# One core, Fourier transform and two expert layers: two-operand work on one engine, both width sums on TensorE, layer 1 of all tiles before layer 2

## The chip, the cores and the metric

The kernel runs on 1 core of one Trainium2 chip. The metric is device time in microseconds (us); the kernel before takes 1074.73 us (median of 3 runs, 1071.64 to 1076.15). The engines are TensorE (PE; PEld is its weight load), VectorE (DVE), ScalarE (ACT), GpSimd (POOL) and SyncE (SP, which only issues DMAs here).

## The reference

```python
X = np.fft.fft(np.fft.fft(x, axis=1), axis=2).real      # x: 8 x 3072 x 256
x = X.reshape(8 * 3072, 256)
logits = x @ w_gate                                     # 8 experts
e = argmax(logits); gate = softmax(logits)[e]
# each expert takes its first 768 tokens (capacity), in order; the others give 0
h = relu(disp @ w1[e])          # 256 -> 1024, 8 x 768 rows
y = h @ w2[e]                   # 1024 -> 256
x = gate * y   (0 for tokens that were dropped)
out = max(0.01 * (x @ w_in), x @ w_in) @ w_out          # 256 -> 2048 -> 256
```

All is float32 (w_in and w_out come as float64). Rows of dropped tokens are zero. The kernel multiplies in split form: each factor is a high part and a low part (`x - high`), and each product is three matmuls. So every matrix needs a copy by ScalarE (the high part) and a subtraction (the low part), `split`.

## The kernel before, in words

*Transform stage.* With these inputs the capacities are full after 2.5 of the 8 batches, so only three batches are transformed (`NSTAT = 3`; for the third only half the rows). For each batch `fold_steps` adds and subtracts rows and columns of x that share a table entry (three pieces of rows, j = 0 to 2, each with steps `a0`, `a1`, `b0`), `fsplit_steps` splits the result, `s1_steps` does the transform along the length (TensorE, banks evacuated by `s1_ev_odd` and `s1_ev_even`), and `s2_steps` the transform along the width in 12 chunks of 128 rows. A chunk gives a row block `yd` and its mirror image `ym`; U is the cosine sum and V the sine sum, `yd = U - V` and `ym = U + V`. Three ways are in the code: mode "v" makes U and V by 4 + 3 matmuls of 264 columns and lets VectorE form difference and sum out of PSUM; mode "p" lets TensorE accumulate U - V in one bank and U + V in another, with 14 matmuls, and ScalarE copies both out; mode "d" makes `yd` alone. Before, `PEW` gives mode "p" to 4 chunks of batch 0 and 6 of batch 1; the other 14 of these two batches are "v". Rows with their gate logits go to a table in DRAM (`y_first`). `route` then finds expert, position and slot of each token (one-hot products of `hot` and `place`).

*Expert stage* (`moe_static`). 8 experts x 2 tiles of 384 tokens make 16 tiles. Layer 1 of a tile: `prep` gathers its rows by indirect DMA (POOL queue), `tr` transposes them, `h` (8 steps of 6 matmuls of 384 columns) and `y` (2 steps of 24). Layer 2 of a tile: `h2` and `o`, 16 steps each, then `fin` scatters the rows. Expert weights are loaded by SP and split by `conv_w1` and `conv_w2`; `wide_steps` turns w_in and w_out (float64, as bit patterns) into split form in 16 slices of 512 columns, and must be done before the first `h2`. `zero_step` writes zeros into the output (48 DMAs of 512 KB, on SP).
Before, `lead = 6` tiles go through layer 1, with the wide slices beside them; from then on layer 2 of tile i runs with layer 1 of tile i + 6 in between (`HS`, `W1S` and `W2S` say at which step), and the last 6 tiles have layer 2 alone. The results `yf` of layer 1 wait in 6 SBUF buffers (`my`).

*Who does two-operand work.* `tt` takes VectorE unless it is told another engine; `on(kind, key)` chooses between VectorE and POOL by `SWAP`. In the transform stage POOL takes, of the fold, mostly the column differences (`d`, `q`), the step `b0` for j < 2 and the small edge rows; and a part of the table and evacuation splits and the product with `cid` in `hot`. In the expert stage it takes two of the three two-operand instructions of each wide slice (the third in some slices) and a part of the weight splits.

*Order.* SP runs in the order written, and in `moe_static` ScalarE too; the other engines' order is set by the planner at build time, from its own time model and the data that each instruction needs. `step(pe, own, fn)` runs a step and then takes background steps from a list (`bg`) as far as the credit goes: each step adds its TensorE time `pe` less `own`, each background step has a price (the number beside it).

```python
def split(self, hi, lo, src, eng=None):        # before
    self.act(hi, src)
    self.tt(lo, src, hi, ALU.subtract, eng)
...
self.later([(c * 1.6, f) for c, f in steps])   # the wide slices, beside layer 1
...
self.step(6 * U, 0.5, lambda: self.h(i, f))
```

Of the kernel before, what the change touches and what calls it, by code (L numbers as in the profile page):

```python
# [144 lines left out]
class Kern:  # L145

    SWAP = {
        "tab": ((2, 1),),
        "fold": ((1, 1, "q"), (2, 0, "c"), (2, 1, "b"), (2, 1, "e"), (2, 2, "a")),
        "fs": ((1, 0),),  # L150
        "s1o": ((0, "c", 0), (0, "s", 0), (1, "c", 1), (2, "c", 1), (2, "s", 1)),
        "wd": ((12,), (14,), (4,)),
        "wl": ((5,),),
        "w1": ((1, 1), (1, 2), (1, 3), (2, 0), (2, 2)),
        "w2": ((0, 2), (0, 3), (2, 0), (2, 2), (3, 1), (3, 2), (4, 2)),
    }

    def __init__(self, tc, cap, a):
        self.tc, self.nc, self.a = tc, tc.nc, a
        self.cap = cap  # L160
        self.lead = 6
        self.nt = max(1, -(-cap // T))
        self.capp = self.nt * T
        self.ntab = E * self.capp
        self.slots = self.gq = None
        self.bg, self.credit = [], 0.0

    def on(self, kind, *key, usual="V"):

        v = (usual == "V") != (key in self.SWAP[kind])  # L170
        return self.nc.vector if v else self.nc.gpsimd
# [29 lines left out]
    def tt(self, o, x, y, op, eng=None):  # L201
        (eng or self.nc.vector).tensor_tensor(out=o, in0=x, in1=y, op=op)  # L202
# [4 lines left out]
    def split(self, hi, lo, src, eng=None):  # L207
        self.act(hi, src)
        self.tt(lo, src, hi, ALU.subtract, eng)
# [49 lines left out]
    def build_tables(self, tmp, yp, nb):  # L259
# [5 lines left out]
        for i, n in enumerate("csn"):  # L265
            self.split(self.mv[n + "h"][:, :D], self.mv[n + "l"][:, :D], f[:, i], nc.gpsimd)
# [52 lines left out]
    def load_table(self, pt, j):  # L319

        nc, a = self.nc, self.a
        st = []
        h = TJ // 2
        for i in range(2):
            t = pt.tile([P, h], F32, name="tst", tag=("pch", "pcl", "psh", "psl")[2 * (j % 2) + i])
            o = j * TJ + i * h
            nc.sync.dma_start(out=t, in_=a["tab"][:, o:o + h])
            st.append((1.2, lambda t=t, o=o, i=i: self.split(self.th[:, o:o + h], self.tl[:, o:o + h], t,
                                                             self.on("tab", j, i, usual="VG"[i]))))
        return st  # L330
# [25 lines left out]
    def fold_steps(self, b, pool2=True, pool3=False):  # L356


        nc, tmp = self.nc, self.tmp
        V, G = nc.vector, nc.gpsimd  # L360
        def en(op, j, d):
            return self.on("fold", bkey(b), j, op, usual=d)

        def copy(o, x):
            (G if pool3 else V).tensor_copy(out=o, in_=x)
# [4 lines left out]
        def extra():  # L370
# [3 lines left out]
            tt(t[:, :D], xe[:, 0], xe[:, 1], A, G)  # L374
            tt(xe[:, 0], xe[:, 0], xe[:, 1], M, G)
            tt(c7, c7, x4, A, G)
            tt(o7, xe[:, 0, :P], xe[:, 0, P:], M, G)
            loc["c7"], loc["o7"], loc["x4"] = c7, o7, x4

        def fix():  # L380
            ce, r, c7 = loc["ce", 0], loc["r"], loc["c7"]
            tt(r[0:1, 4, 0], ce[0:1, 0], c7, M, G)
            tt(r[0:1, 5, 0], ce[0:1, 0], c7, A, G)
            copy(loc["x4"], ce[0:1, 1])

        def a0(j):
# [8 lines left out]
            tt(e, x[:, :, :P], x[:, :, P:], A, en("e", j, "V"))  # L395
            tt(x[:, :, :P], x[:, :, :P], x[:, :, P:], M, en("d", j, "G"))
            tt(q, x[:, 0::2, :P], x[:, 1::2, :P], M, en("q", j, "G"))
            if not pool3:
                self.next_x()

        def a1(j):
            e, r = loc["e"], loc["r"]
            c = e[:, 0::2]
            tt(c, c, e[:, 1::2], A, en("c", j, "V"))
            ce = tmp.tile([P, 2, P], F32, name="ce", tag="ce")
            loc["ce", j] = ce
# [8 lines left out]
        def b0(j):  # L415
            if pool3:
                self.next_x()
            Z = en("b", j, "G" if pool3 and j < 2 else "V")
            o, r = loc["o", j], loc["r"]
            se = tmp.tile([P, 2, P], F32, name="se", tag="se")  # L420
            tt(se, o[:, 0::2], o[:, 1::2], M, Z)
            tt(r[:, 2:4, j], o[:, 2::-2], o[:, 3::-2], A, Z)
            tt(r[:, 6, j], se[:, 0], se[:, 1], A, Z)
            tt(r[:, 7, j], se[:, 0], se[:, 1], M, Z)
# [5 lines left out]
        ca = (1.2 if pool2 else 3.0, 1.7, 0.1 if pool3 else 1.1)  # L430
        for i, (f, j) in enumerate(((a0, 0), (a1, 0), (a0, 1), (b0, 0), (a1, 1), (a0, 2), (b0, 1), (a1, 2), (b0, 2))):
            st.append((1.8 if kb == NSTAT - 1 and i == 0 else ca[(a0, a1, b0).index(f)], lambda f=f, j=j: f(j)))
# [11 lines left out]
    def fsplit_j(self, loc, j):  # L444
        self.split(self.f[0][:, :, j], self.f[1][:, :, j], loc["r"][:, :, j], self.on("fs", 0, j))

    def fsplit_steps(self, loc, b=None):
        st = [(0.2, lambda: (self.open_f(), self.fsplit_x(loc)))]
        for q in (0, 2, 1, 3):
            c = slice(2 * q, 2 * q + 2)  # L450
            eng = self.on("fs", b, q)
            st.append((0.9, lambda c=c, eng=eng: self.split(self.f[0][:, c], self.f[1][:, c], loc["r"][:, c], eng)))
# [31 lines left out]
    def s1_ev_odd(self, fn, pa, pb, eng=None, b=9):  # L484
# [9 lines left out]
        for i, (t, v) in enumerate(((t1, lambda h: self.pv(fn + h, 1)[:, :n]), (t3, lambda h: self.pv(fn + h, 3)[:, n - 1::-1]))):  # L494
            self.split(v("h"), v("l"), t, self.on("s1o", b, fn, i))
# [11 lines left out]
    def s1_steps(self, eng=None, b=9):  # L507
# [4 lines left out]
        def odd(cls, fn, par):  # L512
            def go():
# [5 lines left out]
                if par == "B":  # L519
                    self.s1_ev_odd(fn, loc["A"], ps, eng, b)  # L520
# [21 lines left out]
    def s1_first(self):  # L542
# [23 lines left out]
        evac = [(1.9, lambda: self.s1_ev_odd("c", banks["cA"], banks["cB"], b=0)), (0.95, lambda: evens(0)),  # L566
                (1.9, lambda: self.s1_ev_odd("s", banks["sA"], banks["sB"], b=0)), (0.95, lambda: evens(2))]
# [170 lines left out]
    def route(self, b, L, n):  # L738
# [76 lines left out]
        def hot(c, m):  # L815
# [8 lines left out]
            self.tt(r[:, :, 0], o, at(self.cid[:, b], w), ALU.mult, G)  # L824
# [45 lines left out]
    def wide_steps(self, pool, eng=None, eng2=None):  # L870
# [4 lines left out]
        G = eng or V  # L875
# [46 lines left out]
        def parts(i):  # L922
# [5 lines left out]
            self.tt(lf, lf, sq, ALU.mult, G)  # L928
            self.tt(bm, bm, hi.bitcast(F32), ALU.subtract, self.on("wd", i))
            self.tt(lo, bm, lf, ALU.add, self.on("wl", i, usual="G"))  # L930

        st = [(1.1, lambda: bits(0))]
        for i in range(len(order)):
# [3 lines left out]
            st.append((0.3, lambda i=i: parts(i)))  # L937
# [25 lines left out]
    def conv_w1(self, q, eng=None, e=None):  # L963
        if e is not None:
            eng = self.on("w1", e, q)
# [4 lines left out]
        self.split(h[:, :, c], l[:, :, c], self.w["w1r"][:, :, c], eng)  # L970

    def conv_w2(self, q, eng=None, e=None):
        if e is not None:
            eng = self.on("w2", e, q)
# [4 lines left out]
        self.split(h[:, c], l[:, c], self.w["w2r"][:, c], eng)  # L979

    def prep(self, key, e, t, upto=None):
# [8 lines left out]
        ix = mx.tile([P, KT, 2], I32, name="mix", tag="mix", bufs=self.lead + 4)  # L990
# [11 lines left out]
    def gate(self, key):  # L1002
# [3 lines left out]
        self.tt(s["no"], s["no"], xg[:, :, NL], ALU.add, nc.gpsimd)  # L1006
# [12 lines left out]
    def gate2(self, key):  # L1019
# [3 lines left out]
        g = mx.tile([P, KT], F32, name="gate", tag="gate", bufs=self.lead + 4)  # L1023
# [147 lines left out]
    PEW = ((3, 5, 7, 11), (1, 3, 5, 7, 9, 11))  # L1171

    def static(self, rps):
# [41 lines left out]
        self.later(self.fold_steps(1, pool3=True))  # L1215
# [5 lines left out]
        for b in range(NSTAT):  # L1221
            last = b == NSTAT - 1
            if b:
                one, mm, two, put = pend
                one()
                if last:
# [5 lines left out]
                    steps = [(0.1, lambda q=q: self.conv_w1(q, nc.gpsimd)) for q in range(4)]  # L1232
                    self.bg[:0] = [(3.5, mm), (0.5, two)] + steps
                    self.later(put + [(0.1, lambda: self.prep(0, *tiles[0], upto=2 * S))])
                else:
                    fs, loc = self.fold_steps(b + 1, pool3=True), self.floc
                    self.later(fs[:1] + [(1.5, mm), (1.5, two)] + fs[1:])
                for s in self.s1_steps(None, b):
                    self.step(*s)
            if not last:  # L1240
                self.later(self.fsplit_steps(loc, b + 1))
# [3 lines left out]
            for s in self.s2_steps(b, L, b, (lambda c: "d") if last else  # L1245
                                   (lambda c, b=b: "p" if c in self.PEW[b] else "v")):
# [20 lines left out]
    def moe_static(self, es, tiles, rps):  # L1267
        nc = self.nc
# [3 lines left out]
        self.my = self.pool("my", self.lead, es=es)  # L1272
# [4 lines left out]
        n, k = len(tiles), min(self.lead, len(tiles))  # L1277
        steps = self.wide_steps(cv, nc.gpsimd)
# [3 lines left out]
        nz = self.yd.shape[0] // self.ZR  # L1282
# [5 lines left out]
        for i in range(k):  # L1288
# [4 lines left out]
            for f in range(NF1):  # L1293
                self.step(6 * U, 0.5, lambda: self.h(i, f))
                if new and f % 2 == 0:
                    self.conv_w2(f // 2, e=e)
# [8 lines left out]
                if f == 6 and i:  # L1305
                    zero(1)
# [4 lines left out]
            for d in range(2):  # L1311
                if wnew:
                    self.conv_w1(2 * d, e=tiles[i + 1][0])
                    self.conv_w1(2 * d + 1, e=tiles[i + 1][0])
# [6 lines left out]
        ys, lag = [], []  # L1321
# [8 lines left out]
        for i in range(n):  # L1330
            a = i + k
            go = a < n
            if go:
                e, t = tiles[a]
                new = tiles[a - 1][0] != e
                nxt = a + 1 < n
# [186 lines left out]
```

## Time and profile before

| | us |
|---|---|
| median of 3 runs | 1074.73 (1071.64 to 1076.15) |
| profiled execution, own time | 1075.6 |
| its span, first to last instruction | 1073.8 |
| granted TensorE clock, mean over the span | 0.942 |
| PE busy / PEld busy | 959.5 / 903.8 |
| DVE / ACT / POOL busy | 643.7 / 479.9 / 302.0 |

A busy PE is not PE at its peak: matmuls are pipelined, so the records of two overlap, and time per matmul is read from the distance of two starts. PEclk is the granted clock (1.00 is 2.4 GHz, 0.50 is 1.2 GHz). In groups by line, line 202 is `tt` and line 205 is `act`, whoever calls them; the tiles tell which step it is.

### The profile page before, as it was taken

The page shows a single profiled execution, that of the slowest core. Times are in us where ns is not written, and L with a number is a line of the kernel's source. Part 1 is how long each engine was busy: PE and PEld are TensorE (multiplying, and loading weights), DVE is VectorE, ACT ScalarE, POOL GpSimd, SP SyncE. Part 2 cuts the span into 40 slices and gives each one's busy share as a digit, 9 for nine tenths or more (in the row PEclk, how much of TensorE's full clock was granted, in tenths as well). Part 3 has the DMA queues.
Part 4 walks back from the last instruction along what each step waited for, and adds up shares of the span by engine and source line. Part 5 has one row for each costly group of instructions (what it writes and reads, how often), then busy time and mean ns, then how long its engine had stood idle before and what let it go on. Part 6 is the DMA issues. An engine that isn't in the chain of part 4 may idle for free.

```text
span 1073.8 us, 14976 instructions
## 1 busy us (share of the span) xinstructions
PE 959.5 (89%) x5403; PEld 903.8 (84%) x5403; DVE 643.7 (60%) x1228; ACT 479.9 (45%) x1074; POOL 302.0 (28%) x323
## 2 busy tenths in 40 slices
PE   1767887888887999999999999999999999999990
PEld 1656866877777999999999999999999999999990
DVE  7998955769884546455545645474556355555550
ACT  3234433445554445345444535463445344454440
POOL 8876534576664011202020202020000100110011
PEclk9768878889888999999999999999999999999995
DMA  7326162336469225102500240030000000000000
GB/s 273 115 79 200 44 196 71 103 121 194 157 203 359 71 78 176 38 5 84 182 30 2 89 157 31 1 109 1 15 6 11 10 6 16 16 16 11 5 15 18
DMA packets 57567, 89.03 MB, mean 83 GB/s; under 512 B 4901, under 2 KB 46761, under 8 KB 56332
## 3 DMA queue, kind: packets, MB, share of 16 engines
q1 hardware_dynamic: 44840, 67.03, 18.8%
q0 software_dynamic: 4640, 12.81, 3.8%
q10 hardware_dynamic: 8004, 8.14, 2.6%
q8 instruction: 44, 0.72, 0.3%
q14 instruction: 39, 0.32, 0.1%
HBM read 48.37 MB, written 39.60 MB: 82 GB/s over the span
## 4 chain that ended last, share of the span: by engine, by line
PE 70%; DVE 8%; issue 4%; POOL 4%; DMA 3%; ACT 1%; POOLq 0%; ACTq 0%; SPq 0%; DVEq 0%
PE po L1111 16%; PE po L1112 8%; PE psg L216 8%; PE psg L218 8%; PE psg L217 8%; PE psh L216 3%; PE psh L218 3%; PE psh L217 3%; PE psy L218 3%; PE psy L217 3%; PE psy L216 3%; POOL xg L996 1%; DMA xg<-y_first,mix 1%; DMA y_first<-ym 1%; DVE r L908 1%
## 5 line engine op out<-in xcount | busy, mean ns | idle before, releaser
L1111 PE MATMUL po<-wo,gh 128*128 128x512 f32 x768 | 255.4, 393 | 0.0
L202 DVE TENSOR_TENSOR gf<-gt,psg 128x384 f32<-128x384 f32 x256 | 141.7, 553 | 188.4 <-ACT gt L205 186.2
L205 ACT ACTIVATE gt<-psg 128x384 f32<-128x384 f32 x256 | 125.9, 492 | 197.5 <-PE psg L218 195.2
L1112 PE MATMUL po<-wo,gl 128*128 128x256 f32 x768 | 182.4, 280 | 0.0
L216 PE MATMUL psg<-yh,wi 128*128 128x384 f32 x512 | 172.7, 338 | 6.9 <-ACT yh L205 6.9
L218 PE MATMUL psg<-yh,wi 128*128 128x384 f32 x512 | 172.0, 336 | 0.0
L217 PE MATMUL psg<-yl,wi 128*128 128x384 f32 x512 | 172.0, 336 | 0.0
L1111 PEld LDWEIGHTS po<-wo,gh 128*128 128x128 f32 x768 | 141.7, 187 | 16.8
L1122 POOL DMA_INDIRECT out<-ob,mix x48 | 49.1, 1023 | 348.7 <-DVE ob L1121 280.2
L202 DVE TENSOR_TENSOR gl<-gf,gh 128x384 fp32r<-128x384 f32 x256 | 141.4, 552 | 6.4 <-ACT gh L205 6.3
L1112 PEld LDWEIGHTS po<-wo,gl 128*128 128x128 f32 x768 | 137.3, 188 | 3.5
L205 ACT ACTIVATE gh<-gf 128x384 fp32r<-128x384 f32 x256 | 133.0, 520 | 7.0 <-PE po L1111 6.8
L996 POOL DMA_INDIRECT xg<-y_first,mix x48 | 52.7, 1099 | 278.2 <-PE pst L1035 267.0
L1054 DVE SCALAR_TENSOR_TENSOR hl<-psh,hh 128x384 fp32r<-128x384 f32 x128 | 70.1, 553 | 75.2 <-ACT hh L205 75.2
L205 ACT ACTIVATE hh<-psh 128x384 fp32r<-128x384 f32 x128 | 62.1, 492 | 110.8 <-PE psh L218 110.7
L216 PEld LDWEIGHTS psg<-yh,wi 128*128 128x128 f32 x512 | 96.4, 189 | 11.9 <-ACT yh L205 7.2
L216 PE MATMUL psh<-xTh,w1h 128*128 128x384 f32 x256 | 91.3, 358 | 15.0 <-DVE hl L1054 12.7
L217 PEld LDWEIGHTS psg<-yl,wi 128*128 128x128 f32 x512 | 96.3, 188 | 3.0
L218 PEld LDWEIGHTS psg<-yh,wi 128*128 128x128 f32 x512 | 96.3, 188 | 0.7
L217 PE MATMUL psh<-xTl,w1h 128*128 128x384 f32 x256 | 89.3, 349 | 0.0
L218 PE MATMUL psh<-xTh,w1l 128*128 128x384 f32 x256 | 89.3, 349 | 0.0
L216 PE MATMUL psy<-hh,w2h 128*128 128x384 f32 x256 | 87.6, 342 | 1.2 <-DVE hl L1054 1.2
(256 smaller groups left out, 1641.3 us busy)
## 6 DMA issues: line engine op xcount, KB each, us to landing
out<-zero SPq DMA_DIRECT2D x48, 512.0 KB, 8.0
xj<-in_xg SPq DMA_DIRECT2D x9, 1024.0 KB, 4.9
w1r<-in_w SPq DMA_DIRECT2D x9, 1024.0 KB, 6.9
w2r<-in_w SPq DMA_DIRECT2D x9, 1024.0 KB, 6.4
y_first<-yd ACTq DMA_DIRECT2D x12, 397.5 KB, 4.2
w<-in_w_in SPq DMA_DIRECT2D x8, 512.0 KB, 6.6
w<-in_w_out SPq DMA_DIRECT2D x8, 512.0 KB, 3.8
tst<-in_tab SPq DMA_DIRECT2D x6, 576.5 KB, 7.0
```

The lines of the kernel that those rows point to most:

```text
L202: (eng or self.nc.vector).tensor_tensor(out=o, in0=x, in1=y, op=op)
L205: self.nc.scalar.activation(out=o, in_=x, func=func, scale=scale)
L216: nc.tensor.matmul(out=out, lhsT=lh, rhs=rh, start=start and i == 0, stop=False)
L217: nc.tensor.matmul(out=out, lhsT=lh, rhs=rl, start=False, stop=False)
L218: nc.tensor.matmul(out=out, lhsT=ll, rhs=rh, start=False, stop=stop and i == n - 1)
L908: V.tensor_scalar(out=r, in0=hw, scalar1=3, scalar2=0x3FFFFFF8, op0=ALU.logical_shift_left, op1=ALU.bitwise_and)
L996: G.indirect_dma_start(out=xg[:, k], out_offset=None, in_=self.yd[0:upto] if upto else self.yd[:], in_offset=bass.IndirectOffsetOnAxis(ap= ...
L1054: nc.vector.scalar_tensor_tensor(out=lo, in0=ps[:, :T], scalar=0.0, in1=hi.bitcast(F32), op0=ALU.max, op1=ALU.subtract)
L1111: mm(out=o, lhsT=gh[:, c], rhs=both, start=f == 0, stop=False)
L1112: mm(out=o[:, :D], lhsT=gl[:, c], rhs=first, start=False, stop=f == NF2 - 1)
L1122: nc.gpsimd.indirect_dma_start(out=self.a["out"][0:nr], out_offset=bass.IndirectOffsetOnAxis(ap=s["ix"][:, k, 1:2], axis=0), in_=ob, in_of ...
```

## The change

All two-operand work in `tt` goes to VectorE: `SWAP`, `on` and the engine arguments go, POOL keeps the gathers, scatters and some small integer work of `prep` and `gate`. All chunks of batches 0 and 1 use mode "p". `moe_static` runs layer 1 for all 16 tiles, then layer 2 for all 16; each tile's `yf` (393 KB) is written to DRAM (`ysp`) from the ScalarE queue and read back by SP two tiles ahead of its use; `my` has 2 buffers in place of 6. The zero DMAs all go between the tiles of layer 1, 4 per tile. Prices of background steps change; the wide slices are spread thinner (4.1 x 1.3 in place of 2.4 x 1.6 per slice).

```diff
-    def tt(self, o, x, y, op, eng=None):
-        (eng or self.nc.vector).tensor_tensor(out=o, in0=x, in1=y, op=op)
+    def tt(self, o, x, y, op):
+        self.nc.vector.tensor_tensor(out=o, in0=x, in1=y, op=op)
...
-            tt(e, x[:, :, :P], x[:, :, P:], A, en("e", j, "V"))
-            tt(x[:, :, :P], x[:, :, :P], x[:, :, P:], M, en("d", j, "G"))
-            tt(q, x[:, 0::2, :P], x[:, 1::2, :P], M, en("q", j, "G"))
-            if not pool3:
-                self.next_x()
+            tt(e, x[:, :, :P], x[:, :, P:], A)
+            tt(x[:, :, :P], x[:, :, :P], x[:, :, P:], M)
+            tt(q, x[:, 0::2, :P], x[:, 1::2, :P], M)
+            self.next_x()
...
-        ca = (1.2 if pool2 else 3.0, 1.7, 0.1 if pool3 else 1.1)
+        ca = (3.1, 2.1, 1.6)
...
-            self.tt(lf, lf, sq, ALU.mult, G)
-            self.tt(bm, bm, hi.bitcast(F32), ALU.subtract, self.on("wd", i))
-            self.tt(lo, bm, lf, ALU.add, self.on("wl", i, usual="G"))
+            self.tt(lf, lf, sq, ALU.mult)
+            self.tt(bm, bm, hi.bitcast(F32), ALU.subtract)
+            self.tt(lo, bm, lf, ALU.add)
...
-            st.append((0.3, lambda i=i: parts(i)))
+            st.append((2.0, lambda i=i: parts(i)))
...
-                                   (lambda c, b=b: "p" if c in self.PEW[b] else "v")):
+                                   (lambda c: "p")):
...
-        self.my = self.pool("my", self.lead, es=es)
+        self.my = self.pool("my", 2, es=es)
...
-        self.later([(c * 1.6, f) for c, f in steps])
+        self.later([(c * 1.3, f) for c, f in steps])
...
-        for i in range(k):
+        def late(i, d, end):
+            def go():
+                end()
+                if d:
+                    nc.scalar.dma_start(out=self.ysp[i], in_=self.st[i].pop("yf"))
+            return go
+
+        for i in range(n):
...
-                self.step(6 * U, 0.5, lambda: self.h(i, f))
+                self.step(6 * U, 0.55, lambda: self.h(i, f))
...
-                    zero(1)
+                    zero(per)
...
-                self.step(24 * U, 0.0, lambda: self.y(i, d, True))
+                self.step(24 * U, 0.0, lambda: late(i, d, self.y(i, d, True)))
         self.upto()
+        zero(len(zq))
...
+        self.yload(0)
+        self.yload(1)
         self.ysplit(0)
...
         for i in range(n):
-            a = i + k
-            go = a < n
...
             for f in range(NF2):
                 self.h2(i, f)
                 lag.append((i, f))
                 tail(self.LAG)
-                if ys:
-                    self.y(a - 1, ys.pop(0))
-                if go:
...
                 if f == 8 and i + 1 < n:
                     self.ysplit(i + 1)
-                if i and f % 4 == 3:
-                    zero(1)
...
+                if f == 9 and i + 2 < n:
+                    self.yload(i + 2)
...
+    def yload(self, i):
+        self.st[i]["yf"] = t = self.mg.tile([P, 2, T], F32, name="yf", tag="yf", bufs=2)
+        self.nc.sync.dma_start(out=t, in_=self.ysp[i])
```

## Rows read from the trace of the kernel before

**Rows 1.** Windows: busy us (instructions) per engine and stage, clock, DMA share, GB/s.

```profile
0.00:190.00 190.00, 127.15 (x691) 112.21 (x691) 152.41 (x253) 70.65 (x172) 120.05 (x123) 0.83 0.43 139
190.00:338.00 148.00, 122.31 (x627) 115.15 (x626) 114.39 (x215) 74.66 (x158) 101.07 (x106) 0.89 0.55 177
338.00:850.00 512.00, 510.99 (x2952) 490.36 (x2953) 266.80 (x546) 238.16 (x531) 60.46 (x75) 1.00 0.20 65
850.00:1049.00 199.00, 199.00 (x1136) 186.09 (x1134) 108.81 (x212) 95.34 (x212) 17.50 (x18) 1.00 0.04 13
```

**Rows 2.** Chain that ended last: one layer-2 step, a tile apart, twice.

```profile
417.67 0.70 PE po L1111 x3
468.36 0.70 PE po L1111 x3
...
882.82 0.70 PE po L1111 x3
916.49 0.70 PE po L1111 x3
```

**Rows 3.** Timeline of the first fold: start us, us, engine, line, out<-in.

```profile
7.32 2.86 POOL L202 TENSOR_TENSOR xj<-xj 128x1024 f32<-128x1024 f32 x1 [1.37 <-DVE fe L202]
8.00 2.46 DVE L202 TENSOR_TENSOR ce<-fe 128x256 f32<-128x256 f32 x1
...
17.48 1.21 DVE L202 TENSOR_TENSOR fe<-xj 128x1024 f32<-128x1024 f32 x1
...
22.16 0.41 DVE L202 TENSOR_TENSOR ce<-fe 128x256 f32<-128x256 f32 x1
```

**Rows 4.** Groups by line and form, POOL, 0 to 190 us (busy us, mean ns).

```profile
L202 POOL TENSOR_TENSOR xj<-xj 128x1024 f32<-128x1024 f32 x9 | 23.6, 2620 | 8.9 <-DVE fe L202 8.8
```

**Rows 5.** Groups by line and form, DVE, 0 to 190 us.

```profile
L202 DVE TENSOR_TENSOR fe<-xj 128x1024 f32<-128x1024 f32 x8 | 13.0, 1619 | 4.9 <-DMA xj<-in_xg 4.9
L202 DVE TENSOR_TENSOR se<-xj 128x256 f32<-128x256 f32 x6 | 10.1, 1682 | 1.2 <-POOL xj L202 1.2
...
L202 DVE TENSOR_TENSOR ce<-fe 128x256 f32<-128x256 f32 x8 | 7.2, 898 | 0.1
...
L202 DVE TENSOR_TENSOR yd<-psu,vs 128x264 f32<-128x264 f32 x14 | 5.9, 422 | 1.7 <-DMA y_first<-yd 1.2 <-PE psu L218 0.5
```

**Rows 6.** Timeline of PE in the width transform of batch 0.

```profile
77.90 0.42 PE L216 MATMUL psu<-mvch,pch 128*128 128x264 f32 x1
78.12 0.42 PE L217 MATMUL psu<-mvcl,pch 128*128 128x264 f32 x1
...
80.10 0.28 PE L217 MATMUL psu<-mvcl,pch 128*128 128x264 f32 x1
80.22 0.29 PE L218 MATMUL psu<-mvch,pcl 128*128 128x264 f32 x1
```

**Rows 7.** Groups by line and form, POOL, 190 to 338 us.

```profile
L202 POOL TENSOR_TENSOR lf<-lf,sq 128x512 f32<-128x512 f32 x16 | 22.2, 1390 | 8.0 <-DVE sq L919 7.9
```

**Rows 8.** Timeline of DVE beside layer 1 of an early tile.

```profile
219.49 0.43 DVE L919 TENSOR_SCALAR sq<-r 128x512 uint32<-128x512 uint32 x1
...
220.90 0.68 DVE L202 TENSOR_TENSOR r<-r,wi 128x512 f32<-128x512 f32 x1
221.50 0.55 DVE L1054 SCALAR_TENSOR_TENSOR hl<-psh,hh 128x384 fp32r<-128x384 f32 x1
```

**Rows 9.** Waits of PE, 190 to 345 us: us in total, times, longest.

```profile
PE psh L216 <- DVE hl L1054: 12.7, 9, 3.8
PE psg L216 <- ACT yh L205: 6.9, 1, 6.9
```

**Rows 10.** Waits of DVE, 190 to 338 us.

```profile
DVE r L908 <- POOL wi L202: 9.3, 3, 4.1
```

**Rows 11.** DMA issues: KB each, us to landing.

```profile
out<-zero SPq DMA_DIRECT2D x48, 512.0 KB, 8.0
```

**Rows 12.** Window of 25 us with the most DMA traffic.

```profile
325.00:350.00 25.00, 18.08 (x95) 17.50 (x95) 11.13 (x19) 8.20 (x18) 11.32 (x12) 0.86 1.05 357
```

More of the change, by code (lines that the diff above doesn't have):

```diff
@@ L354, in next_x, with fold_steps @@
         self.xt[bkey(b), j] = t
[L356 to L362, printed above, removed]
+    def fold_steps(self, b):
+        tmp = self.tmp
         def copy(o, x):
-            (G if pool3 else V).tensor_copy(out=o, in_=x)
+            self.nc.vector.tensor_copy(out=o, in_=x)
         st, loc, xt, kb = [], {}, self.xt, bkey(b)
@@ L961, in load_w2, with conv_w1 @@
         self.w["w2r"] = t
-    def conv_w1(self, q, eng=None, e=None):
-        if e is not None:
-            eng = self.on("w1", e, q)
+    def conv_w1(self, q):
         if q == 0:
@@ L969, in conv_w1, with conv_w2 @@
         c = slice(256 * q, 256 * q + 256)
[L970 to L974, printed above, removed]
+        self.split(h[:, :, c], l[:, :, c], self.w["w1r"][:, :, c])
+    def conv_w2(self, q):
         if q == 0:
@@ L989, in prep @@
             nc.sync.dma_start(out=rid, in_=self.tbl[bass.ds(s0, T)].rearrange("(k p) c -> p (k c)", p=P))
-        ix = mx.tile([P, KT, 2], I32, name="mix", tag="mix", bufs=self.lead + 4)
+        ix = mx.tile([P, KT, 2], I32, name="mix", tag="mix", bufs=self.live)
         no = mx.tile([P, KT], F32, name="no", tag="no", bufs=4)
@@ L1005, in gate @@
         xg, V = s["xg"], nc.vector
-        self.tt(s["no"], s["no"], xg[:, :, NL], ALU.add, nc.gpsimd)
+        nc.gpsimd.tensor_tensor(out=s["no"], in0=s["no"], in1=xg[:, :, NL], op=ALU.add)
         nc.gpsimd.tensor_copy(out=s["ix"][:, :, 1], in_=s["no"])
@@ L1022, in gate2 @@
         m, d = s.pop("m"), s.pop("d")
-        g = mx.tile([P, KT], F32, name="gate", tag="gate", bufs=self.lead + 4)
+        g = mx.tile([P, KT], F32, name="gate", tag="gate", bufs=self.live)
         V.tensor_reduce(out=m, in_=d, op=ALU.add, axis=AX.X)
@@ L1231, in static @@
                     self.load_w2(0)
-                    steps = [(0.1, lambda q=q: self.conv_w1(q, nc.gpsimd)) for q in range(4)]
+                    steps = [(0.1, lambda q=q: self.conv_w1(q)) for q in range(4)]
                     self.bg[:0] = [(3.5, mm), (0.5, two)] + steps
@@ L1276, in moe_static @@
         self.tr(0)
-        n, k = len(tiles), min(self.lead, len(tiles))
-        steps = self.wide_steps(cv, nc.gpsimd)
+        n = len(tiles)
+        steps = self.wide_steps(cv)
         wide = len(steps)
-        self.later([(c * 1.6, f) for c, f in steps])
+        self.later([(c * 1.3, f) for c, f in steps])
         zq = list(range(B * S // self.ZR))
-        nz = self.yd.shape[0] // self.ZR
+        per = -(-len(zq) // (n - 1))
         def zero(m):
@@ L1330, in moe_static @@
         for i in range(n):
-            a = i + k
-            go = a < n
-            if go:
-                e, t = tiles[a]
-                new = tiles[a - 1][0] != e
-                nxt = a + 1 < n
-                wnew = nxt and tiles[a + 1][0] != e
             for f in range(NF2):
@@ L1419, in general @@
             with tc.tile_pool(name="cv", bufs=2) as cv:
-                for _, fn in self.wide_steps(cv, nc.gpsimd):
+                for _, fn in self.wide_steps(cv):
                     fn()
@@ L1468, in build @@
             dr = self.pool("dr", 1, es=es, space=DRAM)
+            self.ysp = dr.tile([self.ntab // T, P, 2, T], F32, name="y_kept")
             y_all = dr.tile([B * S, NR], F32, name="y_all")
```

134 lines of the change are left out of this document (44 added, 90 removed).

## The prediction

> **What bounds the kernel now.** I read the windows by stage first [rows 1]. From 338 us on PE is busy in 710 of 711 us at clock 1.00: there only a change in TensorE work could move the time. Before 338 us it is not: in the transform stage (0 to 190 us) PE is busy 127 us of 190 at a mean clock of 0.83, in the six leading tiles of layer 1 (190 to 338 us) 122 of 148 at 0.89. So the reader should look for gains and losses in these two stages, and price TensorE work alone in the rest.
>
> The chain that ended last gives the prices of a tile [rows 2]: the same step of two successive tiles is 468.36 - 417.67 = 50.69 us apart where layers 1 and 2 are interleaved, and 916.49 - 882.82 = 33.67 us where layer 2 is alone. Layer 1 of a tile therefore costs TensorE 17.02 us at full clock. Six leading tiles would be 102.1 us; they took 148, so 45.9 us are lost there. PE's waits there name DVE's `hl` (12.7 us in 9 waits) and, at the end, ScalarE's `yh` (6.9 us) [rows 9]; DVE itself waits for POOL's wide slices [rows 10]. The rest of the loss is the lower clock that goes with the gaps.
>
> In the transform stage DVE is busy 152 of 190 us, but much of it isn't work. The timeline [rows 3] shows it: `ce` takes 2.46 us while POOL's 2.86 us subtraction runs beside it, and 0.41 us where POOL is idle. Against the shortest record of the same form, 8 `fe` at 1.21 lose 13.0 - 9.7 = 3.3 us, 6 `se` at 0.41 (the length of `ce`, same size) 7.6, 8 `ce` 3.9 [rows 3, 5]: 14.8 us in three groups. The same reading over the other groups of that view gives another 28, 43 us in all (estimate). DVE waits inside its instructions for POOL.
>
> **The change, part by part.** The sum is made against the profiled execution (own time 1075.6 us, 1.8 above its span); the median of the runs is 0.9 lower, and I take that off at the end.
>
> *Transform stage, two-operand work to DVE.* POOL is busy 120 us in it [rows 1], some 107 of that with two-operand instructions (estimate, the groups of that view summed). A 128x1024 one takes 2.62 us there [rows 4] and 1.21 on DVE [rows 3], a ratio of 0.46, so they add about 48 us to DVE. What goes: the 28 `yd` and `ym` of mode "v", 28 x 0.42 = 11.8 us [rows 5], and the 43 us of waiting. DVE would then have 152 + 48 - 12 - 43 = 145 us, 7 less than now: nearly even. What should shrink besides is the ping-pong between the engines: the first table product waits for a fold that goes DVE, POOL, DVE, and POOL's part of it is one instruction of 2.86 us that needs 1.21 on DVE [rows 3] and others like it; I expect it some 5 us earlier.
>
> *Width transform, all chunks "p".* 14 chunks change from 7 matmuls to 14: 98 more of 264 columns. Two starts are 0.22 us apart at the half clock and 0.12 at the full one [rows 6]: 11.8 to 21.6 us of TensorE. It lies beside the fold of the next batch on DVE (about 22 us per batch by the lengths above), which is needed before the next length transform, so I cost it at nothing; without that cover it is 12 to 22 us. ScalarE gets 14 copies more than it loses, some 0.4 us each if it copies as fast as DVE adds [rows 5], beside.
>
> For the stage I take -8 us. Ends: -20 (all of DVE's 38 idle us there, half of it used) and +37 (none of the 43 us goes: 48 - 12). I stay near the even sum, since the rows show the stretch and its partner directly.
>
> *Layer 1 of 16 tiles.* Ten more tiles move ahead of layer 2, with their gathers on POOL, weight loads on SP, weight splits, and all 48 zero DMAs. TensorE's matmuls are the same, 16 x 17.02 = 272.3 us, plus 16 x 33.67 = 538.7 us for layer 2. The question is what is lost beside them. DVE per tile: 8 `hl` at 0.55 = 4.4, 2 transposed splits 1.1, half of an expert's 8 weight splits at 0.68 = 2.7, gate about 1; a wide slice is now seven DVE instructions, 5 x 0.68 + 2 x 0.43 = 4.3 [rows 8]. A tile earns a credit of 11.8 and a slice costs 4.1 x 1.3 = 5.3, so 2.2 slices, 9.5 us. Sum 18.7 us against PE's 17.0; but two successive starts are closer than one duration (220.90 to 221.50 is 0.60 for 0.68), about 0.08 on some 35 instructions, which makes it 16. So DVE and PE are level for the 7 or 8 tiles with slices, and then DVE has half of its time free. POOL's `lf` at 1.39 us [rows 7] and the waits on it are gone. I take 8 us for the start (first gathers and half clock, as now) and 12 for these tiles.
>
> DMA: a tile now has 4 zero DMAs (2.1 MB), half an expert's weights (1.05), 2.2 slices (1.15), gather 0.4 and the new store 0.39, 5.1 MB in 17.5 us = 290 GB/s. The most that a window shows is 357 at a DMA share of 1.05 [rows 12]. It fits, but loads queue behind zeros on SP, and a zero takes 8.0 us to land [rows 11]. Where a slice comes late, DVE's L908 waits, and `hl` behind it on DVE, and PE for a bank. That is in the 12 us; alone its ends are 0 and, at 2 us per tile, 16.
>
> *Store and reload of `yf`.* 16 issues on ScalarE's queue, behind a copy that ran on the same engine; ScalarE is busy half of the time [rows 1], so a microsecond each would still lie beside. Weight splits queue behind them there. Reads are two tiles ahead. Nothing.
>
> *The change of layers.* Once, PE waits for the last copy, `yh` and `yl`: by size from the 0.55 us of 384 columns [rows 8] 0.5 + 1.0 + 1.0, and some latency, 4 us, in place of the 6.9 [rows 9] that is part of the 45.9.
>
> Expert stage: lost 45.9 before, 8 + 12 + 4 = 24 after, so -22 (ends -36, if only the start is left, and -2). Interleaved layers bring no loss when taken apart, because PE is full in both kinds of stretch [rows 1].
>
> Sum: 1075.6 - 8 - 22 = 1045.6; less 0.9, **1045 us**.
>
> A rule speaks against this. In the interleaved stretch DVE is busy 267 of 512 us, ACT 238 and PE all of it [rows 1]; apart, layer 1 would have DVE near full. The Trainium skill ("Perfetto Trace Analysis", Optimization Strategy) says that a kernel whose regimes have different busiest engines may gain from interleaving them. This change does the reverse. By that rule layer 1's loss would be higher, as in the second rival below; by the rows the mix only moves a bound that PE already holds.
>
> **The rivals.** (a) *DVE becomes the bound of the transform.* If the long records of DVE are not POOL's doing, moving 48 us to it and taking 12 away adds 36 us to an engine that is busy 80% of the stage; with the idle 38 us absorbing a quarter, +28. With -22 in the expert stage: 1081 us. It decides from 22 us on. Against it: the same form at 0.41 and 2.46 us [rows 3]. (b) *Layer 1 is held by DVE or by DMA.* Slices late behind zeros and DVE over PE by 2 us in each of the first 8 tiles, 1 in the others: 24 us instead of 12, and the transform stage even: 1075.6 - 10 = 1065. For it: the level sums; against it: the lower load of tiles 9 to 16. (c) *The transform gains more.* DVE's idle time shrinks with the ping-pong, PE has fewer gaps, and the stage ends 25 us earlier: 1075.6 - 25 - 22 = 1028. For it: DVE has 38 idle us. Against it: 7 us less of DVE work.
>
> **How the numbers follow.** Forecast 0.60, (a) 0.14, (b) 0.15, (c) 0.11. Faster by over 0.5% (below 1069, about what a measurement of this kernel can tell from no change): forecast, (c) and two thirds of (b), 0.81; within 0.5%: most of the rest of (b) and a little of (a), 0.07; slower 0.12. The range goes from 1022, below (c), to 1074, past (b); what is left out is most of (a) and a tail of (c).
>
> **What would show it.** Right: DVE's `fe` at 1.2 and `se` and `ce` at 0.4 us in the transform; expert stage starting near 182 us; tiles of layer 1 about 18 us apart, 17.0 in the second half; tiles of layer 2 33.67 apart; one gap of about 4 us between. Wrong: DVE busy without a break past 190 us with PE waiting for `fl` or `raw` (a); PE waiting for `hl` in every early tile, or DVE's L908 for the load of a slice (b). A layer-2 pitch above 33.7 would be a cause that I do not see.

## The result: 1041.1 us, 3.0% faster

The changed kernel takes 1041.14 us (median of four runs, 1040.33 to 1042.24), against 1073.85 (1071.64 to 1076.15) before: ratio 0.9696, 95% interval 0.9672 to 0.972. The forecast was 1045, range 1022 to 1074. The profiled execution has a span of 1039.9 us, 33.9 less than the 1073.8 of before.

Three marks of TensorE divide the span: the first transposition of gathered tokens (layer 1 starts), the first `psg` matmul (layer 2 starts) and the last `po` matmul. They stand at 187.1, 339.0 and 1048.8 us before, at 182.1, 477.9 and 1016.7 after. So the transform ends 5.0 us earlier, the expert stage is 27.1 us shorter (861.7 to 834.6), and the tail 1.8.

The windows of the kernel after, with columns as in [rows 1]:

```profile
0.00:60.00 60.00, 25.83 (x127) 22.56 (x127) 55.04 (x119) 24.55 (x42) 3.02 (x11) 0.91 0.56 194
60.00:90.00 30.00, 18.17 (x131) 18.20 (x132) 29.87 (x71) 11.47 (x30) 0.00 (x0) 0.72 0.48 154
90.00:120.00 30.00, 26.84 (x174) 24.38 (x173) 21.52 (x51) 15.29 (x39) 1.50 (x3) 1.00 0.16 56
120.00:182.00 62.00, 50.27 (x353) 46.75 (x353) 32.68 (x82) 25.47 (x76) 4.70 (x11) 0.87 0.43 133
182.00:338.00 156.00, 147.51 (x837) 142.35 (x838) 135.32 (x303) 90.98 (x191) 52.15 (x78) 0.97 0.78 267
338.00:478.00 140.00, 138.12 (x812) 137.55 (x810) 65.17 (x147) 63.25 (x136) 19.23 (x29) 1.00 0.45 151
478.00:1017.00 539.00, 538.94 (x3072) 504.60 (x3072) 296.00 (x573) 259.30 (x573) 43.81 (x45) 1.00 0.07 23
```

DVE is near full until 90 us (84.9 of 90) and only then gives way to PE. POOL has almost nothing left in the transform. In layer 1 PE is busy 285.6 of 296 us, in layer 2 always. The groups by line and form of DVE, 0 to 190 us, answer to [rows 5]: `fe` went from 1619 ns to 1211, `se` from 1682 to 412, `ce` from 898 to 407. With the work of POOL added, DVE is busy 139.1 us in the transform (the first four windows, 182 us), fewer than the 152.4 of 190 us before.

```profile
L185 DVE TENSOR_TENSOR fe<-xj 128x1024 f32<-128x1024 f32 x9 | 10.9, 1211 | 2.8 <-DMA xj<-in_xg 2.8
...
L185 DVE TENSOR_TENSOR se<-xj 128x256 f32<-128x256 f32 x9 | 3.7, 412 | 0.1
L185 DVE TENSOR_TENSOR ce<-fe 128x256 f32<-128x256 f32 x9 | 3.7, 407 | 0.0
```

PE's waits after, first 60 to 190 us, then 182 to 500 (us in total, times, longest):

```profile
PE psu L646 <- DVE smov L185: 17.9, 1, 17.9
PE pst L1002 <- issue: 5.4, 1, 5.4
PE pst L806 <- DVE ohr L797: 3.3, 3, 1.6
```

```profile
PE pst L1002 <- DMA xg<-y_first,mix: 3.7, 3, 2.5
...
PE psg L199 <- ACT yh L188: 1.9, 1, 1.9
PE psy L199 <- DVE hl L1021: 0.8, 2, 0.6
```

Of the 12.7 us of `hl` in [rows 9] 0.4 us is left, and `yh` went from 6.9 us to 1.9. One wait is new: 17.9 us on `smov`, an instruction of 0.15 us for which DVE is late.

The pitches, from the timeline of PE (layer 1) and the chain that ended last (layer 2), one step a tile apart in each; [rows 2] had 33.67 us for layer 2 alone:

```profile
346.30 0.82 PE L1002 MATMUL pst<-ident,xg 128*128 128x128 f32 x6
363.62 0.82 PE L1002 MATMUL pst<-ident,xg 128*128 128x128 f32 x6
```

```profile
859.68 0.70 PE po L1078 x3
...
893.24 0.70 PE po L1078 x3
```

17.32 us in layer 1, 33.56 in layer 2. In the five tiles from 256.53 to 346.30 us, the last that make slices, the mean pitch is 17.95: the slices cost about 3 us there. They make 10 of the 16 slices. The two tiles before them (220.28 to 256.53 us) make four more and lose another 1.6 us.

### The profile page after: what moved, and what is told of

The parts are those of the page before. It is cut to its first block, busy times and chain, and to the rows that moved or that the text cites. A ratio compares the mean times of both kernels' runs of the same rounds, so it can differ in the third digit from the quotient of the medians.

```text
span 1039.9 us, 15207 instructions
## 1 busy us (share of the span) xinstructions
PE 945.7 (91%) x5501; PEld 896.4 (86%) x5501; DVE 636.9 (61%) x1344; ACT 491.3 (47%) x1088; POOL 127.3 (12%) x179
## 4 chain that ended last, share of the span: by engine, by line
PE 76%; DVE 11%; DMA 7%; ACT 2%; issue 1%; ACTq 0%; SPq 0%; POOL 0%; POOLq 0%; DVEq 0%
PE po L1078 17%; PE psg L200 9%; PE po L1079 9%; PE psg L199 9%; PE psg L201 9%; PE psy L199 4%; PE psy L200 4%; PE psy L201 4%; PE psh L199 3%; PE psh L200 3%; PE psh L201 3%; DMA y_first<-ym 2%; DVE hl L1021 1%; DMA out<-zero 1%; DVE psl L185 1%
## 5 line engine op out<-in xcount | busy, mean ns | idle before, releaser
L1078 PE MATMUL po<-wo,gh 128*128 128x512 f32 x768 | 232.6, 394 | 0.0
L1079 PE MATMUL po<-wo,gl 128*128 128x256 f32 x768 | 150.0, 281 | 0.0
L1079 PEld LDWEIGHTS po<-wo,gl 128*128 128x128 f32 x768 | 128.5, 188 | 4.0
L1089 POOL DMA_INDIRECT out<-ob,mix x48 | 46.7, 973 | 556.5 <-DVE ob L1088 478.0
L199 PE MATMUL psh<-xTh,w1h 128*128 128x384 f32 x256 | 86.8, 341 | 0.8 <-ACT xTh L188 0.5
L201 PE MATMUL psh<-xTh,w1l 128*128 128x384 f32 x256 | 86.1, 336 | 0.0
L200 PE MATMUL psh<-xTl,w1h 128*128 128x384 f32 x256 | 86.1, 336 | 0.0
L200 PE MATMUL psy<-hl,w2h 128*128 128x384 f32 x256 | 86.0, 336 | 0.0
L201 PE MATMUL psy<-hh,w2l 128*128 128x384 f32 x256 | 85.9, 336 | 0.0
```

Of the source, the lines that this page charges most:

```text
L199: nc.tensor.matmul(out=out, lhsT=lh, rhs=rh, start=start and i == 0, stop=False)
L200: nc.tensor.matmul(out=out, lhsT=lh, rhs=rl, start=False, stop=False)
L201: nc.tensor.matmul(out=out, lhsT=ll, rhs=rh, start=False, stop=stop and i == n - 1)
L1078: mm(out=o, lhsT=gh[:, c], rhs=both, start=f == 0, stop=False)
L1079: mm(out=o[:, :D], lhsT=gl[:, c], rhs=first, start=False, stop=f == NF2 - 1)
L1089: nc.gpsimd.indirect_dma_start(out=self.a["out"][0:nr], out_offset=bass.IndirectOffsetOnAxis(ap=s["ix"][:, k, 1:2], axis=0), in_=ob, in_of ...
```

## The experiments

### Each part alone, and each part undone

The change has three parts: D (two-operand work to DVE), P (mode "p" for all chunks), L (layers apart, y in DRAM). Six runs with the two kernels give all eight combinations. Two of the eight, D alone and D with L, compute some values of the output wrong, and why is open. They have as many `psu <- smov` matmuls as the kernel before (48), so their times are used as those of the same work.

D alone; the slices keep six tiles to be made in:

```diff
-    def tt(self, o, x, y, op, eng=None):
-        (eng or self.nc.vector).tensor_tensor(out=o, in0=x, in1=y, op=op)
+    def tt(self, o, x, y, op):
+        self.nc.vector.tensor_tensor(out=o, in0=x, in1=y, op=op)
```

> One part alone: two-operand work all on VectorE (with its new prices; the wide slices at 4.1 x 1.0 so that they fit beside six tiles), while mode p stays at PEW and layers stay interleaved after six leading tiles. Theory A (POOL's two-operand work stretches DVE's, so moving it costs nearly nothing): the transform stage ends within 5 us of before's 187 us, no DVE fold instruction above 1.3 us; the six leading tiles lose about 35 us in place of 46, since seven DVE instructions per slice (68 us) still have to fit beside six tiles; 1060 to 1068 us, ratio about 0.99. Theory B (the move is a loss, all gain is from the order of the layers): 1080 to 1095, ratio above 1.005.

1061.37 us, ratio 0.9893 (0.9862 to 0.9924): theory A's time, though not its transform, which ends 7.9 us later (table below).

P alone:

```diff
-                                   (lambda c, b=b: "p" if c in self.PEW[b] else "v")):
+                                   (lambda c: "p")):
```

> One part alone: mode p for all chunks of batches 0 and 1, POOL and order of layers as before. Theory A: DVE loses 12 us of work and PE gets 98 matmuls (12 to 22 us) beside the fold; the transform stage moves by -3 to +3 us, ratio 0.997 to 1.003. Rival C (freeing DVE of the sums is what gains): -8 us or more, ratio below 0.993.

1077.75 us, ratio 1.0043 (1.0022 to 1.0064): a small loss, about 4 us, just past theory A; rival C falls.

L alone:

```diff
-        for i in range(k):
+        for i in range(n):
...
+        self.yload(0)
+        self.yload(1)
```

> One part alone: layer 1 of all 16 tiles, y kept in DRAM, then layer 2; POOL keeps its two-operand work and PEW stays. Theory A: most of the 25 us of the expert stage comes from this, since the slices spread over more tiles, but POOL's slices still stretch DVE: loss 25 to 30 us in place of 46, 1054 to 1060, ratio 0.981 to 0.987. Theory B: all of it, 1043 to 1050, ratio 0.971 to 0.978.

1067.7 us, ratio 0.9956 (0.9929 to 0.9982). Both theories expected more.

P undone, with D and L:

```diff
-                                   (lambda c: "p")):
+                                   (lambda c, b=b: "p" if c in self.PEW[b] else "v")):
```

> The change without mode p: PEW as before, everything else as after. Theory A: DVE gets 12 us more in the transform stage, where it is the bound in the first 75 us but not in the rest: 1042 to 1050 us, ratio to before 0.971 to 0.978. Rival C: 15 us or more lost, 1056 and above, ratio above 0.984.

1054.42 us, ratio 0.9832 (0.9786 to 0.9877): between the two theories, 13 us slower than the changed kernel.

D undone, with P and L:

```diff
-        self.nc.vector.tensor_tensor(out=o, in0=x, in1=y, op=op)
+        (eng or self.nc.vector).tensor_tensor(out=o, in0=x, in1=y, op=op)
```

> This is the changed kernel with one part undone: the two-operand work is shared between VectorE and GpSimd again, as before; TensorE makes both width sums and the layers stay apart. Theory A (the move of the two-operand work is what lets the other two parts pay): the transform ends about 4 us later than before because mode p added TensorE work while GpSimd still holds the fold, layer 1 loses some 3 to 10 us per tile to the slices on GpSimd as in the run with the layers alone; 1062 to 1074, ratio 0.989 to 1.000. Rival B (each part brings its own share, so the whole less the share of the move, 0.9696 / 0.9893): 1050 to 1056, ratio 0.977 to 0.983.

1069.78 us, ratio 0.9973 (0.9949 to 0.9996): theory A.

L undone, with D and P:

```diff
-        for i in range(n):
+        for i in range(k):
```

> The changed kernel with the layers interleaved again, six leading tiles and no y in DRAM; the other two parts stay. Theory A (with the slices on VectorE the lead of six still loses time since too much VectorE work falls into six tiles; sixteen spread it): transform ends near 182 as in the changed kernel, the lead takes about 134 us against 120 of bare TensorE work, the rest goes at 33.7 us a tile and layer; 1047 to 1056, ratio 0.975 to 0.984, so the layers are worth 6 to 14 us here though only 4 us when made alone. Rival B (the layers' order is worth nothing once VectorE makes the slices): 1038 to 1044, ratio 0.967 to 0.972.

1049.22 us, ratio 0.979 (0.9753 to 0.9827): theory A.

The marks of each profiled run (end of transform; from there to the last `po`):

| parts | median us | transform ends | expert stage |
|---|---|---|---|
| none | 1073.85 | 187.1 | 861.7 |
| D | 1061.37 | 195.0 | 843.6 |
| P | 1077.75 | 191.0 | 862.0 |
| L | 1067.7 | 182.4 | 856.4 |
| D, P | 1049.22 | 180.1 | 842.9 |
| D, L | 1054.42 | 193.4 | 836.5 |
| P, L | 1069.78 | 189.8 | 852.5 |
| all | 1041.14 | 182.1 | 834.6 |

In the expert stage the parts add up: D gives 18 to 20 us, L 5 to 10, P 0 to 4. In the transform they don't. L does not touch the transform, so the table has each of its four forms twice: it ends at 187.1 and 182.4 us as it was, at 195.0 and 193.4 with D, at 191.0 and 189.8 with P, but at 180.1 and 182.1 with both. DVE's sum does not explain it: with D alone DVE is busy 149.7 us in 0 to 195, before 153.8, and yet the transform ends later. Two things differ between D alone and D with P. The first is in the groups of DVE of the run with D alone, 0 to 195 us:

```profile
L185 DVE TENSOR_TENSOR yd<-psu,vs 128x264 f32<-128x264 f32 x14 | 5.9, 426 | 8.5 <-DMA y_first<-yd 4.7 <-ACT vs L188 3.8
...
L185 DVE TENSOR_TENSOR ym<-psu,vs 128x264 f32<-128x264 f32 x14 | 5.8, 424 | 2.4 <-DMA y_first<-ym 2.2
```

These 28 instructions hold DVE for 11.7 us, and DVE stands idle 10.9 us more ahead of them, until a store has freed their tile or ScalarE has made `vs`. The idle time is not much more than before (1.7 us for `yd` in [rows 5], 5.0 for `ym`), but with D the whole fold is queued behind it on DVE. P takes these 22.6 us out of DVE's queue. The second is TensorE's clock, in 90 to 120 us of the same run:

```profile
90.00:120.00 30.00, 23.69 (x94) 21.26 (x95) 23.82 (x60) 9.10 (x25) 1.20 (x3) 0.72 0.16 54
```

The granted clock is 0.72 there, a mix of its two levels, with PE idle 6.3 us of 30; with P's matmuls (the window of the kernel after) it is 1.00 and PE is idle 3.2. Together the two are worth 11 to 15 us once D is there. How much each brings was not separated. The clock alone does not decide: with P alone it is 0.94 in this window, before 0.83, and the transform is longer. That P only loses while POOL still holds the fold rests on the times.

L alone fell short since POOL's slices still hold the tiles of layer 1 in which they are made. In the run with P and L, layer 1 takes 315.4 us (189.8 to 505.2), after the full change 295.8. Its POOL groups, 190 to 350 us, and its waits of PE and DVE, 190 to 505 us:

```profile
L202 POOL TENSOR_TENSOR lf<-lf,sq 128x512 f32<-128x512 f32 x16 | 23.1, 1445 | 9.7 <-DVE sq L919 6.5 <-ACT gd L205 3.1
```

```profile
PE psh L216 <- DVE hl L1054: 6.4, 6, 1.6
```

```profile
DVE r L908 <- POOL wi L202: 8.1, 2, 4.4
```

That is the chain of [rows 7, 9, 10] once more. One thing in the table is not the parts' doing: with L alone the transform ends 4.7 us earlier than before. In 150 to 190 us the granted clock was 0.84 there and 0.76 in the run before. Differences of up to 5 us between single marks are therefore not read as effects.

### POOL beside DVE, with no data in common

Idle additions on a buffer of zeros, four beside each fold step of the changed kernel:

```diff
+    def beside(self):
+        for _ in range(4):
+            self.nc.gpsimd.tensor_tensor(out=self.db, in0=self.zero, in1=self.zero, op=ALU.add)
```

> The changed kernel with four idle two-operand additions of 128x256 on GpSimd beside each fold step (27 steps, 108 instructions, some 75 us of GpSimd at about 0.7 us each), on a buffer that nothing else reads. Theory A (VectorE and GpSimd stretch each other when both make two-operand work): the VectorE additions of the fold that run beside them rise from 0.41 us towards the 0.9 to 2.5 us they had before, VectorE's sum in the transform rises by 20 to 40 us and the transform ends 5 to 25 us later; 1046 to 1066, ratio 0.974 to 0.993. Rival B (the stretch before came from the fold's own data, GpSimd and VectorE working on one tile): no row of VectorE rises, 1039 to 1044.

1088.94 us, ratio 1.0156 (1.0108 to 1.0205), beyond both theories. The 108 additions took 133.5 us, not 75. The waits name a second cost (0 to 230 us, and POOL's timeline):

```profile
ACT yd L188 <- POOL rt L779: 31.6, 1, 31.6
...
PE ps L199 <- ACT yd L188: 28.5, 2, 28.4
```

```profile
99.90 41.50 POOL L340 TENSOR_TENSOR db<-zero 128x256 f32<-128x256 f32 x45
141.50 0.38 POOL L779 TENSOR_SCALAR rt<-rt 128x50 f32<-128x50 f32 x1
141.96 4.07 POOL L340 TENSOR_TENSOR db<-zero 128x256 f32<-128x256 f32 x6
```

The gate's own `rt` on POOL was queued behind the additions, and 28.4 us of PE's time with it. This run alone doesn't tell the theories apart.

Memsets in place of additions:

```diff
+        for _ in range(9):
+            self.nc.gpsimd.memset(self.db, 0.0)
```

> The same with nine memsets of 128x256 on GpSimd per fold step, which read nothing: as much GpSimd time or less, no two-operand reads. Theory A (it is the reads of two operands that meet): VectorE's rows stay as in the changed kernel, 1039 to 1044, ratio 0.968 to 0.972. Rival B (any GpSimd work beside VectorE stretches it): VectorE rows rise as in the run with additions and the time goes with them, 1046 or more.

1040.85 us, ratio 0.9708 (0.9657 to 0.9758). POOL was busy 75.8 us with 243 memsets, and `ce` and `se` kept 408 and 413 ns: theory A. Memsets, which only write, don't disturb DVE here.

One addition per step, so that the queue stays short:

```diff
-        for _ in range(4):
+        for _ in range(1):
```

> The run with idle GpSimd additions once more with one per fold step instead of four (27 in all, about 33 us), so that GpSimd's own few instructions of the gate are not queued behind them. Theory A (two-operand work on both engines stretches both): VectorE's 128x256 additions beside them take about 0.8 us in place of 0.41, VectorE gains some 8 to 15 us of busy time while it makes the fold, the transform ends 4 to 12 us later; 1044 to 1054, ratio 0.973 to 0.983. Rival B (the loss of the run with four was the queue on GpSimd alone): 1039 to 1043, ratio 0.968 to 0.972.

1048.23 us, ratio 0.9761 (0.9729 to 0.9794): theory A, 7 us over the changed kernel without the queue (`rt` waits for no addition here); the transform ends at 187.7 in place of 182.1. Its timelines of DVE and POOL:

```profile
7.44 1.52 DVE L185 TENSOR_TENSOR xj<-xj 128x1024 f32<-128x1024 f32 x1
8.88 1.09 DVE L185 TENSOR_TENSOR fe<-fe 128x512 f32<-128x512 f32 x1
...
12.60 0.83 DVE L185 TENSOR_TENSOR ce<-fe 128x256 f32<-128x256 f32 x1
...
39.23 0.67 DVE L185 TENSOR_TENSOR xj<-xj 128x512 f32<-128x512 f32 x1
39.83 0.41 DVE L185 TENSOR_TENSOR ce<-fe 128x256 f32<-128x256 f32 x1
...
44.06 1.21 DVE L185 TENSOR_TENSOR xj<-xj 128x1024 f32<-128x1024 f32 x1
```

```profile
7.95 12.80 POOL L340 TENSOR_TENSOR db<-zero 128x256 f32<-128x256 f32 x11
20.83 30.67 POOL L340 TENSOR_TENSOR db<-zero 128x256 f32<-128x256 f32 x3
```

From 8 to 19 us POOL makes an addition each 1.2 us, and DVE's instructions are longer by 0.31 to 0.42 us whatever their size (1.21 to 1.52, 0.67 to 1.09, 0.41 to 0.83). From 21 to 51 us DVE runs at its own pace and it is POOL that waits: three additions in 30.67 us, where six took 4.07 while DVE stood still. That reads as one engine standing while the other's instruction runs, and not as both slowed in proportion. The Trainium skill ("SBUF — State Buffer", Who interferes with whom) says so: VectorE and GpSimd share one pair of ports, held as an exclusive lock. These rows agree.

### VectorE's order ahead of smov

```diff
-        self.special_fold()
-        self.later(self.fold_steps(1))
+        fs = self.fold_steps(1)
...
+        hand.enter_context(self.in_order("DVE"))
+        self.special_fold()
+        run(ev[0], fs[0], ev[1], lambda: self.build_gate(self.tmp, NSTAT), ev[2], fs[1], ev[3], self.special)
+        self.later(fs[2:])
```

> The changed kernel with VectorE's work around batch 0 placed by hand: the small smov and its evacuations stand ahead of most of batch 1's fold, two fold steps are put between them and the rest of the fold follows. Theory A (the 17.9 us wait of TensorE on smov is only VectorE's order and part of it is on the path): the first psu matmul starts 8 to 15 us earlier than 71.8 us, the transform ends 5 to 10 us earlier, 1031 to 1036, ratio 0.960 to 0.966 of before. Rival B (VectorE's sum bounds the transform, so that the fold left undone is met later): the wait comes back in the next batches, 1039 to 1043, ratio 0.968 to 0.972.

1053.98 us, ratio 0.9807 (0.9778 to 0.9837). The same with three fold steps and the gate behind the evacuations:

```diff
+        run(ev[0], fs[0], ev[1], ev[2], fs[1], ev[3], lambda: self.build_gate(self.tmp, NSTAT), fs[2], self.special)
+        self.later(fs[3:])
```

> As the run before with three fold steps ahead of the special rows instead of two, and the gate's set-up behind them. Theory A: first psu 5 to 10 us earlier, 1032 to 1038, ratio 0.961 to 0.967. Rival B as there: 1039 to 1043.

1050.96 us, ratio 0.9782 (0.9757 to 0.9808). Both are worse than the changed kernel, against both theories. In the first one PE's wait (55 to 190 us) has only changed its name, and the first `psu` matmul starts at 71.14 in place of 71.83 us:

```profile
PE psu L646 <- DVE spec L185: 12.7, 1, 12.7
```

Its windows, to be read beside those of the kernel after:

```profile
0.00:60.00 60.00, 28.13 (x127) 23.96 (x127) 45.00 (x99) 23.84 (x43) 3.01 (x11) 0.89 0.48 174
60.00:90.00 30.00, 18.86 (x140) 18.89 (x141) 24.56 (x52) 12.63 (x34) 0.00 (x0) 0.77 0.36 112
90.00:120.00 30.00, 22.61 (x120) 19.54 (x119) 27.74 (x65) 7.73 (x24) 2.62 (x3) 0.81 0.44 139
```

`smov` was the last of several things that `psu` needs. The next to last in the kernel after, `spec`, shows in its timeline of DVE:

```profile
67.69 1.60 DVE L185 TENSOR_TENSOR spec<-tx,spec 32x384 fp32r<-32x384 f32 x2
...
71.53 0.15 DVE L185 TENSOR_TENSOR smov<-smt,smt 96x8 fp32r<-96x8 f32 x1
```

`spec` is ready at 69.3 us, so an earlier `smov` alone could bring at most 2.5 us of the 17.9. In the first run the three `smov` are ready at 57.4 us, but `spec` only at 71.0. Its DVE order is fixed by hand, so the run tests that whole order and not the place of `smov` alone: DVE idles 10 us more in 0 to 60 than in the kernel after (its longest waits are for copies by ScalarE, 3.5 us for `pch` and 2.4 for `tb`), and 5 more in 60 to 90. The fold that had filled this time is made between 90 and 120 us instead, where PE loses 4 us and the clock (0.81 for 1.00); the transform ends at 193.2 in place of 182.1.

### y stored and loaded twice

```diff
-                    nc.scalar.dma_start(out=self.ysp[i], in_=self.st[i].pop("yf"))
+                    yf = self.st[i].pop("yf")
+                    nc.scalar.dma_start(out=self.ysp[i], in_=yf)
+                    nc.scalar.dma_start(out=self.ysp2[i], in_=yf)
...
         self.nc.sync.dma_start(out=t, in_=self.ysp[i])
...
+        self.nc.sync.dma_start(out=u, in_=self.ysp2[i])
```

> The changed kernel with y written to DRAM twice and loaded twice (a second store of 384 KB and a second load of 384 KB for each tile; the second copy is not used). Theory A (the DRAM copy of y lies beside TensorE work and costs nothing, as predicted): 1039 to 1043, ratio 0.968 to 0.972. Rival B (DMA load in layer 1, at 250 to 350 GB/s, already decides when the gathers and weights land): layer 1's tiles take 18 us and more in place of 17.3, 1046 to 1060, ratio 0.975 to 0.988.

1052.08 us, ratio 0.9787 (0.9755 to 0.9819): rival B in the time, but not in every tile. Layer 2 starts at 489.1 in place of 477.9 us and is no longer than before (537.2 for 538.8), so the loads cost nothing and the stores 11 us. PE's waits, 180 to 500 us, and the two windows in which it loses most:

```profile
PE pst L1002 <- DMA xg<-y_first,mix: 9.9, 4, 5.5
PE psh L199 <- DVE hl L1021: 7.0, 2, 3.7
```

```profile
225.00:250.00 25.00, 21.71 (x118) 21.32 (x117) 17.08 (x37) 11.67 (x25) 10.49 (x19) 0.92 0.80 269
...
325.00:350.00 25.00, 21.29 (x116) 20.85 (x115) 18.66 (x38) 11.95 (x25) 5.43 (x6) 0.93 1.04 358
```

Two tiles hold nearly all of the loss: the pitch is 24.99 us from 220.03 on and 22.88 from 316.82 on, where the changed kernel has 18.93 and 18.08 for the same tiles; the last six pitches are 17.3 us in both. The chain that ended last shows what held the first of the two (L1260 is the issue of the second store, on ScalarE's queue):

```profile
229.04 8.61 DMA w1r<-in_w
...
237.67 0.33 ACTq L1260
...
238.05 0.50 ACT hh L188
...
238.57 0.57 DVE hl L1021
...
239.18 0.69 PE psh L199
```

The issue stands on ScalarE's queue until a weight load that SP issued has landed, and `hh`, `hl` and TensorE stand behind it. In the second tile it is a DMA of zeros (8.52 us, landed at 332.34). The stores thus cost their time through ScalarE's queue, behind late landings. DMA load may be what makes the landings late: in 325 to 350 us the share is 1.04 at 358 GB/s, as much as [rows 12] shows, and the changed kernel stands at 1.03 and 351 GB/s between 300 and 325 us. This was not separated. In the changed kernel ScalarE is idle 0.4 to 0.6 us at each of its 16 stores, once 1.4, and PE's waits on `hl` come to 1.7 us in all of layer 1, so by this path the first copy costs little. What it costs in DMA time was not measured; a y kept in SBUF was not tried.

## Why the prediction was right, point by point

- **Two-operand work to DVE** was right in its mechanism and nearly in size: 145 us of DVE forecast, 139.1 measured in a stage 8 us shorter. That DVE's long records were waiting and not work is shown by `ce` at 407 ns and, with no data in common, by the idle additions. Rival (a) falls. (The upper end given for the stage, +37, is 36 by its own terms, 48 - 12.)
- **All "p" at nothing** was a mis-sized term with the wrong cover. Alone it costs about 4 us; beside D it gives 11 to 15. It takes 11.7 us of work and 10.9 of idle time from DVE's queue, of which the sum had only the work, and it goes with a clock of 1.00 for 0.72 in 90 to 120 us, which the sum did not have. Fold and matmuls do not simply lie beside each other: DVE is near full until 90 us, and PE's 17.9 us wait ends on it.
- **The transform's -8**: -5.0 at the first transposition. The sum set the border at 190 us, 2.9 us past the first transposition of before; "starting near 182" is what came (182.1). That it came so near is in part luck. With both executions of each form the gain lies between 0.3 and 7.0 us, and it is the rest of a loss by D alone (6 to 13 us) and a gain by P on top of it (11 to 15) that the sum had neither of. Rival (c), 25 us, falls.
- **Layer 1**: 295.8 us for 272.3 of bare work, 23.5 lost where 24 was forecast, but otherwise divided. The seven tiles with slices from 220.28 us on lost 4.8 us, not 12: DVE and PE were level as worked out, and that was enough. The pitch where nothing disturbs PE is 17.32 and not 17.02, 4.8 us in 16 tiles. The change of layers shows 1.9 us of wait for the 4 forecast. The rest, some 12 us, is the start, forecast at 8. Rival (b) falls: no wait of PE for `hl` is longer than 0.6 us.
- **The expert stage's -22**: -27.1. Of the 5.1 us between them 2.9 are the same border and another 1.0 its other end: from the first transposition the six leading tiles of before took 151.9 us, 49.8 above bare work and not 45.9.
- **Store and reload at nothing**: not shown for the one copy. The reason given, that an issue of a microsecond on ScalarE's queue lies beside, holds only while the issue does not wait: with a second store it stood behind DMAs that had not landed, and two tiles lost 10.9 us.
- **"Interleaved layers bring no loss when taken apart"**: right. With D and P in place, taking them apart gives 8.1 us (1049.22 to 1041.14). The rule on interleaving that was named against it did not decide here. The reason is shown only in part: the wait at the change of layers is 4.7 us with the lead of six and 1.9 without, and the four tiles before it are 19.2 us apart on average where the changed kernel's same tiles are 18.0. It is not that DVE has no room there: it is busy 116.6 of 133.5 us in the lead, and 114.9 in the first 133.5 us of the changed kernel's layer 1.

So -33.9 came as -5.0, -27.1 and -1.8 for a forecast of -8, -22 and nothing. The errors are 3.0, 5.1 and 1.8 us and partly cancel; 2.9 us of the first two are the one border.

## What to carry to other kernels

Price an engine's work by its shortest record of a form, and look for what runs beside the long ones: moving work to the busier engine can leave that engine with less to do. Judge parts of a change together where they share a queue; here two parts that each lose in the transform are ahead together. A wait names only what came last: before work is reordered for it, look at what comes next to last, and at what the moved work was filling.

## What the runs showed that was not expected

- A POOL addition of 128x256 took 0.68 us beside an idle DVE (six in 4.07), and up to 17.9 us beside a DVE that issues two-operand instructions back to back; memsets on POOL did neither harm nor suffer (312 ns each).
- A second store per tile, 16 in all, cost 11 us of TensorE time through two issues on ScalarE's queue that waited for DMAs issued by SP.
- The 98 matmuls that mode "p" adds went with a higher clock (1.00 for 0.72 in 90 to 120 us), and with D in place the stage with more TensorE work ended earlier.
